# Unused padding tiles in front of the large SBUF tiles of a fused attention and two-MLP kernel

## The chip, the cores and the metric

The kernel runs on one NeuronCore of a Trainium2 chip as one launch. The metric is the device time of that launch in microseconds (us). TensorE (PE in the profile) multiplies, and its weight loads are listed apart as PEld; VectorE (DVE), ScalarE (ACT) and GpSimd (POOL) work on the elements, and SyncE (SP) issues the DMAs. SBUF is the on-chip memory from which the engines read, PSUM the one into which TensorE writes.

## The reference

```python
# 2 batches x 12 heads x 448 tokens x 64, causal
scores = scale * q @ k.T;  scores = where(mask, -1e9, scores)
attn = softmax(scores);    x = attn @ v          # -> x: 896 tokens x 768
h = x @ w_in                                     # 768 x 2048
x = (h * sigmoid(h)) @ w_out                     # 2048 x 768
h = x @ w_in2                                    # 768 x 1024
s = h * softmax(h)                               # over the 1024 features
x = layernorm(s) * g_ln @ w_out2                 # 1024 x 768 -> output 896 x 768
```

All inputs and outputs are float32.

## The kernel before

After the attention come four products, called GEMM1 to GEMM4 here. Each float32 operand is split into a high part and a low part in the type float32r, both four bytes long, and each block product is three matmuls: high by high, and the two mixed ones. A matmul holds one operand in the array as weights (128 rows by 128 columns, the second argument of `nc.tensor.matmul` in this kernel) and streams the other one, the moving operand, past it (128 rows by 256 to 512 columns, the third argument). A weight load of its own (LDWEIGHTS) goes with every matmul, and the profile shows it beside the matmul before it.

- GEMM1 (L295 to L305) has the split weights `wh`, `wl` of `w_in` as array weights, and the attention's result `xh`, `xl` as moving operand, 448 columns for each of the two batches: 16 x 6 x 2 blocks, 576 matmuls. The first 36 of them are issued between pieces of the last heads of the attention (`g1drain`).
- GEMM2 (L479 to L484) has the same ring of weight tiles, and the gated values as moving operand: `gh0`, `gl0` for batch 0 and `gh1`, `gl1` for batch 1, again 448 columns. Its loop takes three blocks (nine matmuls) of batch 0 and then the same three of batch 1; the last four chunks (36 matmuls for each batch) stand apart: first all of batch 0, then all of batch 1. 288 matmuls for each batch.
- GEMM3 (L588 to L597) turns it round: the activations `yh`, `yl` are the array weights, and the whole split matrix `w3h`, `w3l` in SBUF is moving, 512 columns. Seven token tiles of 36 matmuls, 252 in all. Behind each tile, the softmax and layer norm of it run on DVE and ACT.
- GEMM4 (L641 to L652) has transposed activations `lh`, `ll` as array weights and `w4h`, `w4l` as moving operand: 288 matmuls of 384 columns, and in the last token tile 24 of 512 and 24 of 256 columns. The transposes (L630) of a later token tile stand between.

Instructions stand on each engine in the order in which the program is written (`manual_schedule`). The stream of weights is converted and split by ACT, DVE and POOL into a ring of four pairs of tiles ahead of TensorE (`feed_to`, `conv_a`, `conv_b`, `split_w`).

Tile pools lay their tiles one behind the other in each partition of SBUF. Strides and block offsets of all four products are multiples of 256 bytes (448 columns are 1792 bytes, 128 columns 512 bytes, 384 columns 1536 bytes, 768 columns 3072 bytes), so the start of an operand modulo 256 is the same for every block of a product. These are the starts that the built program has:

| product | moving, start mod 256 | weights, start mod 256 | weights minus moving, mod 256 |
|---|---|---|---|
| GEMM1 | `xh`, `xl` 160 | `wh`, `wl` 160 | 0 |
| GEMM2, batch 0 | `gh0`, `gl0` 224 | `wh`, `wl` 160 | 192 |
| GEMM2, batch 1 | `gh1`, `gl1` 160 | `wh`, `wl` 160 | 0 |
| GEMM3 | `w3h`, `w3l` 224 | `yh`, `yl` 160 | 192 |
| transposes of GEMM4 | `ident` 128 | `e` 224 | 96 |
| GEMM4 | `w4h`, `w4l` 160 | `lh`, `ll` 224 | 64 |

The tiles of batch 0 (`gh0`, `gl0`) and `w3h`, `w3l` lie in pools at the right-hand end of SBUF, the others at the left.

Of the kernel before, what the change touches and what calls it, by code (L numbers as in the profile page):

```python
# [8 lines left out]
F32 = mybir.dt.float32  # L9
# [34 lines left out]
def fused(ctx, tc, qT, kT, vv, vt, w1, w2, w3, w4, gl, out):  # L44
# [3 lines left out]
    def pool(name, bufs=1, **kw):  # L48
        return tc.alloc_tile_pool(name=name, bufs=bufs, **kw)

    const = pool("const")
    act = pool("act")
    raw = pool("raw", RAWS)
    xs = pool("xs", XS)
    wring = pool("wring", 4)

    ident = const.tile([128, 128], F32, name="ident")
    xh = act.tile([128, KD, T], F32R, name="xh", tag="ah")
    xl = act.tile([128, KD, T], F32R, name="xl", tag="al")
    g_h, g_l = [None, None], [None, None]  # L60

    with tc.manual_schedule():
# [169 lines left out]
        def split_w(n, c, dst=None, lo_engine=None):  # L232
            x = wx.pop((n, c))
            if dst is None:
                h = wring.tile([128, CH], F32R, name="wh", tag="wh")
                l = wring.tile([128, CH], F32R, name="wl", tag="wl")
                wsp[n, c] = (h, l)
            else:
                h, l = dst
            nc.scalar.activation(h, x, AF.Copy)  # L240
            (lo_engine or nc.gpsimd).tensor_tensor(l, x, h.bitcast(F32), ALU.subtract)  # L241
# [65 lines left out]
        def silu(f, b):  # L307
            ps = gps.pop((f, b))
            sg = sgr.tile([128, S], F32, name="sg", tag="sg")
            nc.scalar.activation(sg, ps[:, :S], AF.Sigmoid)  # L310
            nc.vector.tensor_tensor(sg, ps[:, :S], sg, ALU.mult)
            nc.vector.tensor_copy(g_h[b][:, f], sg)  # L312
            nc.gpsimd.tensor_tensor(g_l[b][:, f], sg, g_h[b][:, f].bitcast(F32), ALU.subtract)  # L313
# [133 lines left out]
        silu(0, 0)  # L447
        silu(1, 0)
        g1p = pool("g1")
        g_h[1] = g1p.tile([128, KF, S], F32R, name="gh1", tag="gh")  # L450
        g_l[1] = g1p.tile([128, KF, S], F32R, name="gl1", tag="gl")
        psd = pool("psd", 2, space=PS)
# [33 lines left out]
        def evict2(ps, d, b):  # L486
            sl = slice(b * S, b * S + S)
            nc.scalar.activation(yh[:, d, sl], ps[:, :S], AF.Copy)
            nc.vector.tensor_tensor(yl[:, d, sl], ps[:, :S], yh[:, d, sl].bitcast(F32), ALU.subtract)
# [3 lines left out]
        def block2(m, b):  # L493
            d, f = divmod(m, KF)
            if f == 0 and b == 0:
                if d < KD - 1:
                    yps[d, 0], yps[d, 1] = pair()
                else:
                    for z in range(B):
                        yps[d, z] = gm.tile([128, 512], F32, name="ps", tag="gm")  # L500
            mm2(yps[d, b], d, f, b)
            return d if f == KF - 1 else None
# [24 lines left out]
        w3p = pool("w3", side="right")  # L527
        w3h = w3p.tile([128, KD * DF2], F32R, name="w3h", tag="h")
        w3l = w3p.tile([128, KD * DF2], F32R, name="w3l", tag="l")
        for m in range(N3):  # L530
            if m == 10:
                for a in tail:
                    block2(a, 1)
                evict2(yps[KD - 1, 1], KD - 1, 1)
            sl = slice(CH * m, CH * m + CH)
            split_w(3, m, (w3h[:, sl], w3l[:, sl]), nc.vector if m % 3 else nc.gpsimd)
# [2 lines left out]
        wring.release()  # L539

        w4p = pool("w4")
        w4h = w4p.tile([128, KF2, DM], F32R, name="w4h", tag="h")
        w4l = w4p.tile([128, KF2, DM], F32R, name="w4l", tag="l")
        dp = pool("dp", 2)

        gain = dp.tile([128, KF2], F32, name="gain", tag="gain", bufs=1)
        nc.sync.dma_start(gain, gl)
# [136 lines left out]
        w4p.release()  # L684
        w3p.release()
        gm.release()
        xs.release()
        raw.release()
        act.release()
# [38 lines left out]
```

## Time and profile before

| | |
|---|---|
| time, median of 3 runs | 449.2 us (448.37 to 449.21) |
| the profiled execution, its own time | 449.83 us |
| its span, first to last instruction | 448.1 us |
| TensorE busy | 440.0 us, 98% |
| VectorE busy | 320.9 us, 72% |
| granted TensorE clock, mean | 0.999 of 2.4 GHz |

The profile is of one execution. Matmuls overlap in the records: a matmul of 448 columns is drawn some 0.37 us long, but the next one starts after some 0.2 us. What a matmul costs is therefore the distance from its start to the start of the next one; it is called its pitch below. The views give starts to 0.01 us, so a pitch is taken over runs of many matmuls.

### The profile page before, as it was taken

Reading aid. Unit: us, or ns where it says so; the run is one execution under the profiler, and the core shown is the slowest. Engines: PE = TensorE matmul, PEld = TensorE weight load, DVE = VectorE, ACT = ScalarE, POOL = GpSimd, SP = SyncE. Lnnn points to the kernel's source line nnn. Section 1 sums busy time; section 2 is a strip of 40 time slices with the busy share of each in tenths; the row PEclk is TensorE's granted clock in tenths of the full one; section 3 lists DMA queues with packets and bytes.
Section 4 is the critical chain, followed back from the end, with each engine's and each line's share of the span. In section 5 each row is a group of like instructions: output and inputs, shape, how many; then the busy total and the mean of one; then the engine's idle time right before and its main releaser. Section 6 shows DMA issues by size and latency. Waiting matters only on the chain.

```text
span 448.1 us, 6969 instructions
## 1 busy us (share of the span) xinstructions
PE 440.0 (98%) x2379; PEld 383.6 (86%) x2379; DVE 320.9 (72%) x705; ACT 223.6 (50%) x519; POOL 168.3 (38%) x197
## 2 busy tenths in 40 slices
PE   8899999999999999999999999999999999999997
PEld 5676767689999999999999999999888888999996
DVE  4988987679999888887785969756878787511110
ACT  4999898354353434344344344433647765712121
POOL 3756664147776656564422424332500000000000
PEclk9999999999999999999999999999999999999999
DMA  5777310205243333333745647464023210010101
GB/s 163 208 244 216 90 37 37 72 27 157 100 140 106 108 95 117 108 106 90 243 126 176 184 149 236 151 198 119 23 71 105 83 60 1 33 39 35 55 35 54
DMA packets 26387, 49.22 MB, mean 110 GB/s; under 512 B 6128, under 2 KB 13936, under 8 KB 26352
## 3 DMA queue, kind: packets, MB, share of 16 engines
q1 hardware_dynamic: 26352, 48.77, 35.2%
q8 instruction: 19, 0.31, 0.3%
q14 instruction: 16, 0.13, 0.1%
HBM read 46.01 MB, written 2.75 MB: 109 GB/s over the span
## 4 chain that ended last, share of the span: by engine, by line
PE 91%; ACT 4%; DVE 4%; issue 0%; DVEq 0%; ACTq 0%
PE h L304 8%; PE h L305 8%; PE h L303 8%; PE h L483 7%; PE h L482 7%; PE h L484 7%; PE ps L650 4%; PE ps L652 4%; PE ps L651 4%; PE h L595 4%; PE h L597 4%; PE h L596 4%; PE pv L186 4%; PE tr L158 3%; ACT e L135 3%; PE sa L118 2%
## 5 line engine op out<-in xcount | busy, mean ns | idle before, releaser
L241 POOL TENSOR_TENSOR wl<-wx,wh 128x384 fp32r<-128x384 f32 x64 | 75.4, 1178 | 102.1 <-ACT wh L240 101.0
L240 ACT ACTIVATE wh<-wx 128x384 fp32r<-128x384 f32 x64 | 33.4, 522 | 77.5 <-PE h L304 37.7
L209 ACT ACTIVATE wr<-wr 128x384 f32<-128x384 f32 x96 | 52.5, 553 | 30.4 <-DMA wr<-w_in 30.4
L220 DVE SCALAR_TENSOR_TENSOR wx<-wr,wx 128x384 uint32<-128x384 uint32 x96 | 65.6, 684 | 0.0
L303 PE MATMUL h<-xh,wh 128*128 128x448 f32 x174 | 64.0, 368 | 0.0
L304 PE MATMUL h<-xl,wh 128*128 128x448 f32 x174 | 64.0, 368 | 0.0
L305 PE MATMUL h<-xh,wl 128*128 128x448 f32 x174 | 64.0, 368 | 0.0
L230 DVE TENSOR_SCALAR wr<-wr 128x384 uint32<-128x384 uint32 x96 | 59.9, 624 | 2.8 <-DMA wr<-w_in 2.7
L214 DVE SCALAR_TENSOR_TENSOR wx<-wr 128x384 uint32<-128x384 uint32 x96 | 59.1, 615 | 1.3 <-POOL gl L313 1.3
L483 PE MATMUL h<-gl,wh 128*128 128x448 f32 x160 | 58.5, 366 | 0.0
L482 PE MATMUL h<-gh,wh 128*128 128x448 f32 x160 | 58.5, 365 | 0.0
L484 PE MATMUL h<-gh,wl 128*128 128x448 f32 x160 | 58.2, 364 | 0.0
L313 POOL TENSOR_TENSOR gl<-sg,gh 128x448 fp32r<-128x448 f32 x32 | 41.2, 1288 | 21.2 <-DVE gh L312 11.3
L135 ACT ACTIVATE e<-e,st 128x384 f32<-128x384 f32 (+3 forms) x84 | 43.6, 523 | 8.3 <-DVE st L129 8.3
L145 POOL TENSOR_TENSOR e<-e,st 128x384 f32<-128x384 f32 (+3 forms) x63 | 37.5, 631 | 26.9 <-PE tr L158 16.6
L650 PE MATMUL ps<-w4h,lh 128*128 128x384 f32 (+2 forms) x112 | 38.3, 342 | 0.0
L651 PE MATMUL ps<-w4l,lh 128*128 128x384 f32 (+2 forms) x112 | 37.8, 338 | 0.0
L652 PE MATMUL ps<-w4h,ll 128*128 128x384 f32 (+2 forms) x112 | 37.8, 337 | 0.0
L639 DVE TENSOR_TENSOR ll<-tp,lh 128x512 fp32r<-128x512 f32 x14 | 9.0, 686 | 38.0 <-ACT lh L638 38.0
L304 PEld LDWEIGHTS h<-xl,wh 128*128 128x128 f32 x174 | 32.7, 188 | 3.4
L303 PEld LDWEIGHTS h<-xh,wh 128*128 128x128 f32 x174 | 32.7, 188 | 3.3
L305 PEld LDWEIGHTS h<-xh,wl 128*128 128x128 f32 x174 | 32.7, 188 | 3.2
(100 smaller groups left out, 845.0 us busy)
## 6 DMA issues: line engine op xcount, KB each, us to landing
wr<-w_in SPq DMA_DIRECT2D x96, 384.0 KB, 3.5
k<-kT_in SPq DMA_DIRECT2D x12, 224.0 KB, 2.8
q<-qT_in SPq DMA_DIRECT2D x12, 192.0 KB, 3.0
v<-vv_in SPq DMA_DIRECT2D x12, 192.0 KB, 2.9
out<-o SPq DMA_DIRECT2D x12, 192.0 KB, 1.9
qt<-qT_in SPq DMA_DIRECT2D x24, 16.0 KB, 2.5
v<-vt_in SPq DMA_DIRECT2D x12, 32.0 KB, 2.5
out<-o SPq DMA_DIRECT2D x1, 256.0 KB, 2.0
```

Of the source, the lines that this page charges most:

```text
L135: nc.scalar.activation(ep(p, u), ep(p, u), AF.Exp, bias=st[p][:, 0, n:n + 1], scale=-1.0, accum_out=st[p][:, 1, n:n + 1])
L214: nc.vector.scalar_tensor_tensor(x.bitcast(U32), r[:, :, 1], 0x80000000, r[:, :, 0], ALU.bitwise_and, ALU.bitwise_or)
L220: nc.vector.scalar_tensor_tensor(xu, r[:, :, 1], 3, xu, ALU.logical_shift_left, ALU.bitwise_or)
L230: nc.vector.tensor_scalar(low, low, 29, None, ALU.logical_shift_right)
L241: (lo_engine or nc.gpsimd).tensor_tensor(l, x, h.bitcast(F32), ALU.subtract)
L303: nc.tensor.matmul(ps[:, :S], wh, rh, start=k == 0, stop=False)
L304: nc.tensor.matmul(ps[:, :S], wh, rl, start=False, stop=False)
L305: nc.tensor.matmul(ps[:, :S], wl, rh, start=False, stop=k == KD - 1)
L482: nc.tensor.matmul(ps[:, :S], wh, rh, start=f == 0, stop=False)
L483: nc.tensor.matmul(ps[:, :S], wh, rl, start=False, stop=False)
L484: nc.tensor.matmul(ps[:, :S], wl, rh, start=False, stop=f == KF - 1)
L650: nc.tensor.matmul(ps[:, :w], lh[:, k], w4h[:, k, ns], start=k == 0, stop=False)
```

## The change

A helper `pad` allocates a tile that nothing writes or reads, so that the tiles behind it in the pool start later. No instruction, no wait and no order on any engine differs between the two programs; only addresses do. A pool `gap` is added so that the tiles behind `xh`, `xl` keep their starts modulo 256 (the raw and converted weights, `wr` and `wx`, move by 64 bytes).

```diff
--- before.py
+++ after.py
@@ -52,9 +52,16 @@
     act = pool("act")
     raw = pool("raw", RAWS)
     xs = pool("xs", XS)
+    gap = pool("gap")
     wring = pool("wring", 4)
 
     ident = const.tile([128, 128], F32, name="ident")
+
+    def pad(where, count):
+        where.tile([128, count // 4], F32, name="pad", tag="pad", bufs=1)
+
+    pad(act, 64)
+    pad(gap, 192)
     xh = act.tile([128, KD, T], F32R, name="xh", tag="ah")
     xl = act.tile([128, KD, T], F32R, name="xl", tag="al")
     g_h, g_l = [None, None], [None, None]
@@ -447,6 +454,7 @@
         silu(0, 0)
         silu(1, 0)
         g1p = pool("g1")
+        pad(g1p, 64)
         g_h[1] = g1p.tile([128, KF, S], F32R, name="gh1", tag="gh")
         g_l[1] = g1p.tile([128, KF, S], F32R, name="gl1", tag="gl")
         psd = pool("psd", 2, space=PS)
@@ -527,6 +535,7 @@
         w3p = pool("w3", side="right")
         w3h = w3p.tile([128, KD * DF2], F32R, name="w3h", tag="h")
         w3l = w3p.tile([128, KD * DF2], F32R, name="w3l", tag="l")
+        pad(w3p, 192)
         for m in range(N3):
             if m == 10:
                 for a in tail:
@@ -539,9 +548,11 @@
         wring.release()
 
         w4p = pool("w4")
+        pad(w4p, 96)
         w4h = w4p.tile([128, KF2, DM], F32R, name="w4h", tag="h")
         w4l = w4p.tile([128, KF2, DM], F32R, name="w4l", tag="l")
         dp = pool("dp", 2)
+        pad(dp, 192)
 
         gain = dp.tile([128, KF2], F32, name="gain", tag="gain", bufs=1)
         nc.sync.dma_start(gain, gl)
@@ -684,6 +695,7 @@
         w4p.release()
         w3p.release()
         gm.release()
+        gap.release()
         xs.release()
         raw.release()
         act.release()
```

The built program's starts with it:

| product | moving, start mod 256 | weights, start mod 256 | distance before | distance now |
|---|---|---|---|---|
| GEMM1 | 224 | 160 | 0 | 192 |
| GEMM2, batch 0 | 224 | 160 | 192 | 192 |
| GEMM2, batch 1 | 224 | 160 | 0 | 192 |
| GEMM3 | 32 | 224 | 192 | 192 |
| transposes of GEMM4 | 128 | 0 | 96 | 128 |
| GEMM4 | 0 | 0 | 64 | 0 |

The tiles of the attention itself keep their distances.

## Rows read from the trace of the kernel before

**Rows 1.** The page: busy time; the chain that ended last; groups (busy, mean ns | idle).
```profile
PE 440.0 (98%) x2379; PEld 383.6 (86%) x2379; DVE 320.9 (72%) x705; ACT 223.6 (50%) x519; POOL 168.3 (38%) x197
...
PE 91%; ACT 4%; DVE 4%; issue 0%; DVEq 0%; ACTq 0%
...
L303 PE MATMUL h<-xh,wh 128*128 128x448 f32 x174 | 64.0, 368 | 0.0
...
L482 PE MATMUL h<-gh,wh 128*128 128x448 f32 x160 | 58.5, 365 | 0.0
```

**Rows 2.** Busy time by stretch: GEMM1's start and middle, GEMM2, GEMM3, GEMM4.
```profile
core 0: us, PE busy (x) PEld busy (x) DVE busy (x) ACT busy (x) POOL busy (x), PEclk, DMA share, GB/s
...
94.00:114.00 20.00, 20.00 (x98) 18.17 (x97) 19.75 (x30) 8.55 (x18) 14.67 (x12) 1.00 0.39 119
130.00:190.00 60.00, 60.00 (x292) 54.51 (x291) 52.80 (x83) 24.25 (x50) 38.12 (x33) 1.00 0.36 111
205.00:315.00 110.00, 110.00 (x543) 101.57 (x542) 82.75 (x153) 45.34 (x90) 37.59 (x32) 1.00 0.56 171
321.00:380.00 59.00, 59.00 (x260) 48.09 (x260) 45.78 (x101) 36.56 (x63) 5.11 (x7) 1.00 0.19 61
381.00:445.00 64.00, 63.87 (x379) 62.38 (x377) 11.49 (x21) 18.52 (x34) 0.93 (x2) 1.00 0.12 42
```

**Rows 3.** Timeline of PE in GEMM1: start us, us, instruction; nine matmuls apart.
```profile
149.97 0.37 PE L303 MATMUL h<-xh,wh 128*128 128x448 f32 x1
...
151.83 0.37 PE L303 MATMUL h<-xh,wh 128*128 128x448 f32 x1
```

**Rows 4.** Timeline of PE in GEMM2's loop: where the batch changes.
```profile
249.63 0.37 PE L482 MATMUL h<-gh,wh 128*128 128x448 f32 x1
...
251.49 0.36 PE L482 MATMUL h<-gh,wh 128*128 128x448 f32 x1
...
253.29 0.37 PE L482 MATMUL h<-gh,wh 128*128 128x448 f32 x1
```

**Rows 5.** Timeline of PE in GEMM2's last four chunks: batch 0, batch 1, GEMM3's first.
```profile
306.39 0.36 PE L482 MATMUL ps<-gh,wh 128*128 128x448 f32 x1
...
313.59 0.37 PE L482 MATMUL ps<-gh,wh 128*128 128x448 f32 x1
...
321.03 0.39 PE L595 MATMUL h<-w3h,yh 128*128 128x512 f32 x1
```

**Rows 6.** Timeline of PE in the attention's last pieces: GEMM1's second nine, to a transpose.
```profile
83.08 0.36 PE L303 MATMUL ps<-xh,wh 128*128 128x448 f32 x1
...
84.90 0.27 PE L158 MATMUL tr<-ident,e 128*128 128x128 f32 x1
```

**Rows 7.** Timeline of PE in GEMM3: begin of tiles 2, 3, 4, 6; last tile's second matmul.
```profile
329.28 0.39 PE L595 MATMUL h<-w3h,yh 128*128 128x512 f32 x1
...
337.53 0.40 PE L595 MATMUL h<-w3h,yh 128*128 128x512 f32 x1
...
345.93 0.40 PE L595 MATMUL h<-w3h,yh 128*128 128x512 f32 x1
...
362.73 0.40 PE L595 MATMUL h<-w3h,yh 128*128 128x512 f32 x1
...
371.12 1.04 PE L630 MATMUL tp<-ident,e 128*128 128x128 f32 x8
...
372.23 0.40 PE L596 MATMUL h<-w3l,yh 128*128 128x512 f32 x1
...
380.26 0.27 PE L630 MATMUL tp<-ident,e 128*128 128x128 f32 x1
```

**Rows 8.** Timeline of PE in GEMM4: nine apart at 384, 512 and 256 columns.
```profile
385.90 0.34 PE L650 MATMUL ps<-w4h,lh 128*128 128x384 f32 x1
...
387.49 0.34 PE L650 MATMUL ps<-w4h,lh 128*128 128x384 f32 x1
...
436.38 0.39 PE L650 MATMUL ps<-w4h,lh 128*128 128x512 f32 x1
...
438.48 0.39 PE L650 MATMUL ps<-w4h,lh 128*128 128x512 f32 x1
...
443.01 0.28 PE L650 MATMUL ps<-w4h,lh 128*128 128x256 f32 x1
...
444.03 0.28 PE L650 MATMUL ps<-w4h,lh 128*128 128x256 f32 x1
```

**Rows 9.** Timeline of POOL and PE where GEMM1's third output block (f = 2) begins.
```profile
97.11 1.14 POOL L241 TENSOR_TENSOR wl<-wx,wh 128x384 fp32r<-128x384 f32 x1
...
100.16 0.37 PE L305 MATMUL h<-xh,wl 128*128 128x448 f32 x1
```

## The prediction

> **What bounds the kernel now.** I read the page first, for the bound: TensorE is busy 440.0 of 448.1 us, and the chain that ended last runs through PE for 91% of the span; the other engines hold it only inside the attention [rows 1]. So from GEMM1 on, time can only go or come by what a matmul costs on TensorE. A busy share doesn't say that, since a matmul's record overlaps the next one's. The second view, busy time by stretch, says it by counts: in GEMM1's middle, 60 us touch 292 matmuls (the first two began earlier), so about one in 207 ns; GEMM2 fits 543 into 110 us, about one in 203 ns, although its matmuls have the same 448 columns [rows 2]. The granted clock is 1.00 in all these stretches, the level of 2.4 GHz, so no clock explains the difference.
>
> The third view, the timeline of PE alone, shows where it comes from. In GEMM1 nine matmuls take 1.86 us: a pitch of 206.7 ns [rows 3]. In GEMM2's loop the nine of batch 1 take 1.86 us too, and the nine of batch 0 behind them 1.80 us: 200.0 ns [rows 4]. It is the same line with the same ring of weights, the same shape, and the page has no idle time before such a line [rows 1]; what differs is the tile that is streamed. The last four chunks repeat it in long runs: 36 matmuls of batch 0 take 7.20 us (200.0 ns), the 36 of batch 1 behind them 7.44 us (206.7 ns) [rows 5]. The table of starts puts a number on the tiles: batch 0 begins 64 bytes off the weights modulo 256 (distance 192), batch 1 and all of GEMM1 at the same residue (distance 0). The program before thus holds a trial of the change in itself.
>
> **The change part by part.** Nothing is added to any engine, no wait is new, nothing is moved past anything. Only starts change, so each product is priced by matmuls times difference in pitch.
>
> GEMM1 goes from distance 0 to 192, with exactly the residues of GEMM2's batch 0 (224 moving, 160 weights). Of its 576 matmuls 540 run back to back and set the end; 540 x 6.7 ns = 3.6 us less. The 36 at the start lie between pieces of the attention. There the pitch at distance 0 is irregular and lower, 1.82 us for nine or 202.2 ns [rows 6], so they would give between 36 x 2.2 and 36 x 6.7 ns, 0.1 to 0.2 us, and less where the attention's chain waits for other engines; I take 0.
>
> GEMM2's batch 1 goes from 0 to 192: 288 x 6.7 ns = 1.9 us less. Batch 0 stays as it is.
>
> Can the weights follow? The tightest place is early in GEMM1: from 94 to 114 us DVE, which converts them, is busy 19.75 of 20 us [rows 2]. The split that feeds the third output block ends at 98.25 us, and TensorE first reads it at 100.16 us: 1.9 us to spare [rows 9]. Until there TensorE has issued the first two blocks of both batches, 72 matmuls, worth at most 72 x 6.7 = 0.5 us, so the cover holds with 1.4 us left. In GEMM1's middle DVE is busy 52.80 of 60 us, in GEMM2 82.75 of 110 [rows 2]: room for a TensorE that is 3% faster. If the cover fails from 94 to 130 us, the gain of that stretch is lost, 36 us / 206.7 ns = 174 matmuls, 1.2 us. That end lies inside the range.
>
> GEMM3 keeps its distance of 192, though both starts change. It has two pitches in itself: its 36 matmuls take 8.25 us in tiles one and two, 8.40 and 8.39 us in tiles three and six (four and five are like them), and in the last tile 35 take 8.03 us: 229.2, 233.3 and 229.4 ns [rows 5, 7]. No address differs modulo 256 between these tiles, so the pitch also depends on how the stream came into step. Taken as it is: 0. All tiles at the low pitch would give 144 x 4.1 ns = 0.6 us, all at the high one would cost 108 x 4.1 ns = 0.4 us.
>
> GEMM4 goes from 64 to 0, a distance that the trace shows only at 448 columns. At 64 the pitch is 176.7 ns for 384 columns (1.59 us for nine), 233.3 for 512 and 113.3 for 256 [rows 8]. Half way between 384 and 512, 448 columns would take 205.0 ns at distance 64, against 206.7 at distance 0 [rows 3]; by that the change costs 1.7 ns x 336 = 0.6 us. From the other side: the 256-column matmuls run at 113.3 / 256 = 0.443 ns a column, and 384 columns at that rate take 170.0 ns, 6.7 less, so 288 x 6.7 = 1.9 us to win if distance 0 lets them. Both rows lie equally far (one differs in distance, the other in width), so I take the middle, 0.7 us less. As far ends I keep the whole difference that distance made in GEMM2, either way: 336 x 6.7 = 2.3 us. The 56 transposes in front go from 96 to 128; at 6.7 ns each that is 0.4 us either way, and I take 0.
>
> A rule of the Trainium skill speaks against all of it. "TensorE: Matmul & The Clock Gate", in "Step-by-step: what each phase is for", says that TensorE reads streamed operand and weights through two independent ports, and that loading the next weights doesn't take read bandwidth from the running matmul. By it the sum would be 0, and the same page, in "Wait — 56ns, not 53.3ns?", gives a pitch of columns over 2.4 GHz plus some 2.5 ns; my estimate from that is 189 ns for 448 columns. The trace agrees with neither: 200.0 and 206.7 ns stand side by side [rows 4].
>
> The sum: 3.6 + 1.9 + 0.7 = 6.2 us less. The profiled execution took 449.83 us, 1.7 of it around its span of 448.1; it would take 443.6. It lies 0.6 us above the median of the three runs, 449.2, so for a median the forecast is 443.0 us.
>
> **The rivals.**
>
> First, GEMM1 falls out of step. GEMM3's third tile shows that a stream at distance 192 can change to a higher pitch and stay there, here over four tiles [rows 7], which in GEMM1 would mean 206.7 ns as before. Against it: the longest run at 192 with 448 columns, 36 matmuls, holds 200.0 ns without a break, and every group of nine begins with it at once [rows 4, 5]. Left are GEMM2's 1.9 and GEMM4's 0.7 us: 446.6.
>
> Second, the distance isn't the cause. `gh0` and `gl0` lie at the right-hand end of SBUF, `gh1`, `gl1`, `xh` and `xl` at the left, so the trial in the trace also compares places. Then padding does nothing: 449.2. Against it speaks that `w3h`, `w3l` lie on the right as well and show both pitches [rows 7]. This is also where the rule of the skill leads.
>
> Third, slower: the high pitch is the state into which any unbroken stream settles, and GEMM2's batch 0 is low only because a stream at another distance ends every nine matmuls before it. With one distance for both batches nothing breaks the stream any more, and from the first tens of matmuls GEMM2's batch 0 takes 206.7 ns: 288 x 6.7 = 1.9 us more. The rest of GEMM3 settles too (0.4), and GEMM4 pays its 0.6: 2.9 us in all, 452.1. For it speaks that GEMM1 is irregular and lower at its start [rows 6] and steady at 206.7 later; against it, the unbroken 36 [rows 5]. It decides if a stream needs more than 36 matmuls to settle.
>
> Fourth, GEMM4 gains more than the bound, because distance 0 suits 384 columns better than 192 suits 448: each further nanosecond there is 0.3 us, and the time falls below 440.
>
> **How the numbers follow.** Forecast with its bounds, 78%; fourth rival, 4%; first, 7%; second, 6%; third, 5%. The low end of the range: 3.6 + 1.9 + 0.2 (the first 36) + 2.3 (GEMM4) + 0.6 (GEMM3) + 0.4 (transposes) = 9.0 us less, 440.2, and 440.0 with half of the spread of the runs, 0.4 us. The high end: GEMM1 and GEMM2 as counted (5.5), GEMM4 2.3 and GEMM3 0.4 worse: 2.8 us less, 446.4. The 18% outside are the second and third rival, the fourth, and most of the first. A measurement of this kernel can tell about 0.2% (0.9 us) from no change. Forecast, first and fourth rival lie beyond that: faster 89%; within it the second, 6%; slower the third, 5%.
>
> **What the profile after would show.** Nine matmuls of GEMM1 in 1.80 us instead of 1.86, at any place from 95 us on; no difference between GEMM2's batches; GEMM2 beginning 3.6 us earlier than now, GEMM3 5.5. In GEMM4 nine matmuls of 384 columns between 1.53 and 1.61 us, with 1.59 meaning that distances 0 and 64 are alike. The count of instructions and the waits of PE in GEMM1 and GEMM2 (none now) stay. The forecast is wrong if GEMM1 still takes 1.86 us for nine (first or second rival, which GEMM2's batch 1 tells apart), if batch 0 rises to 1.86 (third), or if idle time appears in front of PE in GEMM1, which would mean that the split weights come late.

## The result and the profile after

The changed kernel takes 442.5 us (median of four runs, 442.3 to 443.0), the one before 449.0 us beside it: a ratio of 0.986, 95% interval 0.9842 to 0.9877. The forecast was 443.0 us. The profiled execution went from 449.83 to 442.50 us, its span from 448.1 to 440.7.

Timeline of PE in the changed kernel, which answers to [rows 3, 5] (L310 is the former L303, L490 the former L482, L606 the former L595): first two rows 45 matmuls apart in GEMM1, then the last four chunks of GEMM2.

```profile
144.76 0.36 PE L310 MATMUL h<-xh,wh 128*128 128x448 f32 x1
...
153.76 0.36 PE L310 MATMUL h<-xh,wh 128*128 128x448 f32 x1
...
300.76 0.36 PE L490 MATMUL ps<-gh,wh 128*128 128x448 f32 x1
...
307.96 0.36 PE L490 MATMUL ps<-gh,wh 128*128 128x448 f32 x1
...
315.16 0.39 PE L606 MATMUL h<-w3h,yh 128*128 128x512 f32 x1
```

9.00 us for 45 is 200.0 ns, where GEMM1 had 206.7; both batches take 7.20 us for 36, where batch 1 had 7.44. The same view at the borders of the stages, in the kernel before and then in the changed one (first matmul of GEMM1 and of GEMM2; first of GEMM4 and the last of all; GEMM3's first is in the fence above and in [rows 5]):

```profile
74.14 0.47 PE L303 MATMUL ps<-xh,wh 128*128 128x448 f32 x1
...
203.91 0.36 PE L482 MATMUL h<-gh,wh 128*128 128x448 f32 x1
...
381.05 0.42 PE L650 MATMUL ps<-w4h,lh 128*128 128x384 f32 x1
...
444.60 0.28 PE L652 MATMUL ps<-w4h,ll 128*128 128x256 f32 x1
```

```profile
73.88 0.47 PE L310 MATMUL ps<-xh,wh 128*128 128x448 f32 x1
...
199.96 0.36 PE L490 MATMUL h<-gh,wh 128*128 128x448 f32 x1
...
374.55 0.42 PE L661 MATMUL ps<-w4h,lh 128*128 128x384 f32 x1
...
437.28 0.28 PE L663 MATMUL ps<-w4h,ll 128*128 128x256 f32 x1
```

| stretch | before, us | after, us | gain | forecast |
|---|---|---|---|---|
| attention, to GEMM1's first | 74.14 | 73.88 | 0.3 | 0 |
| GEMM1 | 129.77 | 126.08 | 3.7 | 3.6 |
| GEMM2 | 117.12 | 115.20 | 1.9 | 1.9 |
| GEMM3 and its transposes | 60.02 | 59.39 | 0.6 | 0 |
| GEMM4 to its last matmul | 63.55 | 62.73 | 0.8 | 0.7 |

The 0.3 us of the attention can't be told from its spread: in the fourteen traces of this case GEMM1's first matmul starts between 73.2 and 74.9 us.

Busy time by stretch, early GEMM1, its middle, and GEMM2, against [rows 2]: 302 matmuls stand in GEMM1's 60 us instead of 292, and DVE's share there rose from 52.80 to 56.55 us, since the same conversions now have less time.

```profile
94.00:114.00 20.00, 20.00 (x102) 18.75 (x101) 19.75 (x30) 8.30 (x18) 14.93 (x12) 1.00 0.40 119
130.00:190.00 60.00, 60.00 (x302) 56.24 (x301) 56.55 (x88) 25.68 (x54) 41.96 (x35) 1.00 0.40 119
205.00:310.00 105.00, 105.00 (x527) 98.42 (x526) 80.25 (x150) 42.78 (x87) 35.93 (x29) 1.00 0.58 173
```

The tightest feed, against [rows 9]: the split now ends at 97.95 us (96.81 + 1.14) and is first read at 99.56: 1.6 us to spare instead of 1.9.

```profile
96.81 1.14 POOL L248 TENSOR_TENSOR wl<-wx,wh 128x384 fp32r<-128x384 f32 x1
...
99.56 0.36 PE L312 MATMUL h<-xh,wl 128*128 128x448 f32 x1
```

### The profile page after: what moved, and what is told of

Read it like the earlier page. It is cut to its first block, busy times and chain, and to the rows that moved or that the text cites. A ratio compares the mean times of both kernels' runs of the same rounds, so it can differ in the third digit from the quotient of the medians.

```text
span 440.7 us, 6969 instructions
## 1 busy us (share of the span) xinstructions
PE 432.4 (98%) x2379; PEld 382.2 (87%) x2379; DVE 321.9 (73%) x705; ACT 223.5 (51%) x519; POOL 170.3 (39%) x197
## 4 chain that ended last, share of the span: by engine, by line
PE 91%; ACT 4%; DVE 4%; issue 0%; DVEq 0%; ACTq 0%
PE h L312 8%; PE h L311 8%; PE h L310 8%; PE h L492 7%; PE h L491 7%; PE h L490 7%; PE ps L663 4%; PE ps L661 4%; PE ps L662 4%; PE h L608 4%; PE h L607 4%; PE h L606 4%; PE pv L193 4%; PE tr L165 3%; ACT e L142 3%; PE sa L125 2%
## 5 line engine op out<-in xcount | busy, mean ns | idle before, releaser
L248 POOL TENSOR_TENSOR wl<-wx,wh 128x384 fp32r<-128x384 f32 x64 | 77.6, 1212 | 95.4 <-ACT wh L247 91.8
L227 DVE SCALAR_TENSOR_TENSOR wx<-wr,wx 128x384 uint32<-128x384 uint32 x96 | 66.6, 694 | 0.0
L311 PE MATMUL h<-xl,wh 128*128 128x448 f32 x174 | 63.1, 362 | 0.0
L310 PE MATMUL h<-xh,wh 128*128 128x448 f32 x174 | 62.6, 360 | 0.0
L490 PE MATMUL h<-gh,wh 128*128 128x448 f32 x160 | 57.6, 360 | 0.0
L310 PEld LDWEIGHTS h<-xh,wh 128*128 128x128 f32 x174 | 32.5, 187 | 2.3
```

Source lines behind the costliest of these rows:

```text
L227: nc.vector.scalar_tensor_tensor(xu, r[:, :, 1], 3, xu, ALU.logical_shift_left, ALU.bitwise_or)
L310: nc.tensor.matmul(ps[:, :S], wh, rh, start=k == 0, stop=False)
L311: nc.tensor.matmul(ps[:, :S], wh, rl, start=False, stop=False)
L490: nc.tensor.matmul(ps[:, :S], wh, rh, start=f == 0, stop=False)
```

## The experiments

All but the two timed ones are single profiled runs, read by their pitches: the mean time from a matmul's start to the next one's, over a product or a batch in the trace, steps from one batch to the other taken in. The longer steps where a tile of GEMM3 or GEMM4 begins are left out. GEMM1's means take in its irregular first 36 matmuls: 206.5 ns there is 206.7 from 110 to 190 us. The granted clock is 0.999 or 1.000 of 2.4 GHz in every trace. The edits of the sizes are to the changed kernel; "224/160" below means a stream that starts at 224 and weights at 160, modulo 256.

**Shift both.** `gap` and the padding of `g1p` go, `xh` stays moved (not shown in the cut: GEMM4's paddings become 32 and 128).

```diff
     pad(act, 64)
-    pad(gap, 192)
...
-        pad(g1p, 64)
```

> The padding in front of xh stays, but the weights ring and gh1 move by the same 64 bytes: GEMM1 and both batches of GEMM2 stream from residue 224, as in the changed kernel, at distance 0. Theory (the distance decides): 206.7 ns in GEMM1 and in both batches, so batch 0, the one that was low before the change, rises from 200.0 too; GEMM2 is 1.9 us longer than before, the whole kernel 1 to 2 us slower than before less what GEMM3 and GEMM4 give. Rival (the residue 224 of the streamed tile decides): 200.0 in all three. Rival (the place of gh0 decides): batch 0 at 200.0, the others at 206.7. GEMM3 keeps its residues of the changed kernel (32 and 224, distance 192): if its low pitch belongs to them, all seven tiles take 229 ns; if chance brings it in step, some tiles may take 233. GEMM4 stands at 192: if 192 is the best distance whatever the width, its 384 columns take less than 173.5 ns; if the best distance hangs on the width, more.

Batch 0 rose, so neither its place nor the residue of the stream made its 200 ns. But the pitch is 202.6 ns, not 206.7, in all three; 445.2 us. The rows are the tail of GEMM2: 7.29 and 7.30 us for 36.

```profile
303.10 0.36 PE L488 MATMUL ps<-gh,wh 128*128 128x448 f32 x1
...
310.39 0.36 PE L488 MATMUL ps<-gh,wh 128*128 128x448 f32 x1
...
317.69 0.40 PE L604 MATMUL h<-w3h,yh 128*128 128x512 f32 x1
```

GEMM3 ran at 229.0 ns in all seven tiles, apart from two steps of 0.32 and 0.34 us where the third begins, GEMM4 at 173.2 for 384 columns.

**Two sweeps of distances.** Sizes of the paddings in bytes, not program lines, in the order act, gap, g0 (a new padding behind `gl0`), g1, w3, w4, dp.

```diff
-64, 192,   0,  64, 192, 96, 192   # changed kernel
+64,  64, 224, 128,   0, 96,  64   # first sweep
+64, 128,  96,  96,  64, 96, 224   # second sweep
```

> Distances that no run has shown: GEMM1 at 64, GEMM2 batch 0 at 32, batch 1 at 128, GEMM3 at 0, GEMM4 at 128. Theory A (only a near-equal start clashes): GEMM1 and batch 1 at 200 ns or less, batch 0 between 200 and 206.7, GEMM3 at 233 or more, GEMM4 at 173 or less. Theory B (the pattern repeats every 128 bytes, so that 128 is like 0 and 64 like 192): GEMM1 200, batch 1 206.7, GEMM4 at 128 like at 0, 173.5. If neither holds, each distance has a pitch of its own and 256 is the period.

> The rest of the sweep: GEMM1 at 128, GEMM2 batch 0 at 224, batch 1 at 160, GEMM3 at 64, GEMM4 at 32. The distance theory wants GEMM1 here to have the pitch that batch 1 has at 128 in the run before it (within 0.3 ns), although other tiles are streamed. Theory A: all three at or below 203 ns. Theory B: GEMM1 206.7, batch 0 like a distance of 96. GEMM4 at 32 lies between 173.5 (at 0) and 176.7 (at 64) if the pitch changes smoothly.

| distance | 448 columns, ns (stream/weights) | 512 columns, GEMM3 | 384, GEMM4 | 256, GEMM4 |
|---|---|---|---|---|
| 0 | 206.7 (160/160), 202.6 (224/224) | 227.1 | 173.7 | 119.7 |
| 32 | 203.3 (0/32) | | 173.8 | 118.0 |
| 64 | 202.2 (224/32) | 233.3 | 176.7 | 113.8 |
| 128 | 204.0 (224/96), 203.4 (160/32; 204.0 in the unbroken 36) | | 176.0 | 118.4 |
| 160 | 205.7 (192/96) | | | |
| 192 | 200.0 (224/160) | 229.0 | 173.2 | 117.8 |
| 224 | 206.1 (128/96) | | | |

Neither theory A nor B holds: there is no single clash point, 128 isn't like 0, and the order differs by width (0 is the best of the three at 512 columns and, from 160/160, the worst of all at 448; 64 is the best at 256 columns only). At 384 columns 0, 32 and 192 are not to be ranked: behind the first six or so steps of a tile all three run at 173.3 ns. GEMM1 alone, streaming from 224, had 202.2, 204.0, 200.0 and 202.6 ns with weights at 32, 96, 160 and 224: with the stream's start kept, the start of the weights moves its pitch.

Over the whole of batch 1 the distance theory misses its test at 128 (203.4 ns against GEMM1's 204.0, with 0.3 allowed). But that is a broken stream: batch 0, at another distance, stands between every nine of its matmuls. In its unbroken 36 batch 1 settles on 204.0, GEMM1's pitch, from other starts, and so at 128 the theory stands. Thirty matmuls take 6.12 us in both, batch 1 (first sweep) first, then GEMM1 (second):

```profile
311.68 0.37 PE L491 MATMUL ps<-gh,wh 128*128 128x448 f32 x1
...
317.80 0.37 PE L491 MATMUL ps<-gh,wh 128*128 128x448 f32 x1
```

```profile
146.14 0.36 PE L310 MATMUL h<-xh,wh 128*128 128x448 f32 x1
...
152.26 0.36 PE L310 MATMUL h<-xh,wh 128*128 128x448 f32 x1
```

**192 elsewhere.** The same distance from other starts, 160/96 in GEMM1 and GEMM2.

```diff
-    pad(act, 64)
...
+        pad(g0p, 64)
...
-        pad(w3p, 192)
...
-        pad(w4p, 96)
+        pad(w4p, 160)
```

> Distance 192 everywhere in GEMM1 and GEMM2, but from other starts: 160 streamed and 96 for the weights, where all 200.0 ns so far came from 224 and 160. Theory (the distance decides): 200.0 ns in GEMM1 and in both batches. Rival (the pair of starts decides, as distance 0 at 160 and 160 with 206.6 and at 224 and 224 with 202.6 suggests): another pitch, 202 to 207.

200.0 ns in GEMM1 and in both batches; 441.8 us. At 192 the distance did decide, for both pairs of starts tried.

```profile
144.11 0.36 PE L309 MATMUL h<-xh,wh 128*128 128x448 f32 x1
...
153.11 0.36 PE L309 MATMUL h<-xh,wh 128*128 128x448 f32 x1
```

**GEMM1 undone**, four timed runs.

```diff
-    pad(act, 64)
-    pad(gap, 192)
...
-        pad(w3p, 192)
```

> GEMM1's part of the change undone (distance 0, both starts at 160 as before), the rest kept, and GEMM3 at the starts of before (224 and 160). If the starts decide: GEMM1 at 206.6 ns again, both batches of GEMM2 at 200.0, 3.6 us more than the changed kernel, 446.1 us. If GEMM1's 206.7 before was a state that it fell into by chance: 202.6 ns as at 224 and 224, 443.9 us. GEMM3: if its high pitch before was bound to its starts, tiles three to six take 8.40 us again; if it came from how the stream came into step, it may take 8.25 in all.

446.5 us, ratio to before 0.9949 (0.9929 to 0.9969): GEMM1 was back at 206.5 ns, both batches stayed at 200.0. Its median lies 4.0 us above the changed kernel's, for the 3.6 us at which GEMM1 was priced; the spread of its four runs is 1.3. All five traces with GEMM1 at 160/160 have this pitch, and all four at distance 192 have 200.0, so it isn't a state that one execution fell into. Here 45 matmuls take 9.30 us:

```profile
146.81 0.37 PE L308 MATMUL h<-xh,wh 128*128 128x448 f32 x1
...
156.11 0.37 PE L308 MATMUL h<-xh,wh 128*128 128x448 f32 x1
```

GEMM3, at its starts of before, settled on 229.0 ns in every tile: its high pitch of [rows 7] is no property of its starts. The third tile still took 8.35 us, by a step of 0.34 us at its begin, but the next two 8.24 each and not 8.40.

```profile
335.59 0.50 PE L603 MATMUL h<-w3h,yh 128*128 128x512 f32 x1
335.93 0.39 PE L604 MATMUL h<-w3l,yh 128*128 128x512 f32 x1
```

**Distance 0 at two more starts.** All of GEMM1 to GEMM3 at 192/192 and at 96/96.

```diff
-64, 192,   0, 64, 192,  96, 192   # changed kernel
+32,   0,  32,  0,  32,  64, 192   # 192/192
+192,  0, 128,  0, 128, 160, 192   # 96/96
```

> Distance 0 in GEMM1, GEMM2 and GEMM3 with all starts at 192. So far distance 0 had 206.5 ns with starts at 160 (three kernels) and 202.6 with starts at 224 (one). If the starts modulo 64 matter (160 and 224 are both 32 past a multiple, 192 is one), a third pitch is possible; if distance 0 simply has two states, one of the two is seen, 202.6 or 206.5. GEMM3 at distance 0: 227 ns as in the two runs with starts at 224, if the distance decides.

> Distance 0 with all starts at 96, which is 32 past a multiple of 64 like 160 and 224. If the pair of starts modulo 128 decided, 96 would be like 224 and take 202.6 ns; if distance 0 has two states, 202.6 or 206.5, and the stages of one run need not agree. GEMM3 at 227 ns if the distance decides.

At 192/192 GEMM1 had 206.5 ns and both batches 206.7 (450.0 us), at 96/96 all three 202.7 (444.9 us); GEMM3 227.2 and 227.0. With 160 and 224 that fits a rule by starts modulo 128 (96 there: 202.6; 32 and 64: 206.7), on four starts and no more. The tails, first 192/192, then 96/96:

```profile
308.09 0.37 PE L489 MATMUL ps<-gh,wh 128*128 128x448 f32 x1
...
315.53 0.37 PE L489 MATMUL ps<-gh,wh 128*128 128x448 f32 x1
```

```profile
303.20 0.37 PE L489 MATMUL ps<-gh,wh 128*128 128x448 f32 x1
...
310.50 0.36 PE L489 MATMUL ps<-gh,wh 128*128 128x448 f32 x1
```

**Standing reads**, on the kernel before: the weights alone, the stream alone, both (the cut shows both lines; each of the first two runs has one of them).

```diff
             wh, wl = wblock(2, d * KF + f)
+            wh, wl = (a[:, :1].to_broadcast([128, 128]) for a in (wh, wl))
             rh, rl = g_h[b][:, f], g_l[b][:, f]
+            rh, rl = (a[:, :1].to_broadcast([128, S]) for a in (rh, rl))
```

> The kernel before, but GEMM2's weight loads read the first of the 128 columns 128 times over (step 0), so that they stay at one address; starts are those of before. It computes other values from GEMM2 on. Theory (the weight read, walking through SBUF, meets the walking stream): the pitches of the batches, 200.0 and 206.7, both change, and come to within 1 ns of each other if the walk alone makes the clash. Rival (what counts is when a load starts, not what it reads): 200.0 and 206.7 as before.

> The kernel before, but in GEMM2 the stream reads its first column 448 times over (step 0) while the weight loads walk as before; other values from GEMM2 on. If the clash needs two walking reads or a walking stream, both batches lose their excess over 186.7 ns (448 columns at 2.4 GHz), to 190 or less. If the stream's own start address decides alone, 200.0 and 206.7 stay. If a walking weight load meets a standing stream now and then, something between, and the same in both batches.

> Both reads of GEMM2 stand still: stream and weight load each read one column over and over, in batch 0 at starts 192 apart modulo 256, in batch 1 at the same start modulo 256; other values from GEMM2 on. Theory (the memory is divided by address modulo 256, and two reads of one part at once cost time): batch 1 pays most, above 206.7 ns, batch 0 nothing, below 192. Rival (no such division; the excess is a cost of stepping into the stream): both batches alike.

Weights standing: 203.6 ns in batch 0, 206.0 in batch 1; both changed, but the excess stayed and the batches came no closer than 2.4 ns. Stream standing: 189.2 ns in batch 0 and 189.1 in batch 1, and the same again with both standing. So it is the walking stream that loses time. That two standing reads at the same start lose nothing was against the theory of a divided memory as I put it; it doesn't refute one, if a stream that stays on one column needn't read the memory anew for each, which no run here tells. Stream standing, the two tails (6.81 us for 36 each):

```profile
299.26 0.35 PE L483 MATMUL ps<-gh,wh 128*128 128x448 f32 x1
...
306.07 0.35 PE L483 MATMUL ps<-gh,wh 128*128 128x448 f32 x1
...
312.88 0.40 PE L596 MATMUL h<-w3h,yh 128*128 128x512 f32 x1
```

These three kernels leave GEMM4 as it was, and show a second pitch there at unchanged starts (160/224, distance 64): in each, the first of the six tiles of 384 columns settles on 173.3 ns, the other five on 176.7, where the kernel before had 176.7 in all six. Eighteen matmuls with the stream standing in GEMM2, in the first tile and then in the second:

```profile
376.52 0.34 PE L651 MATMUL ps<-w4h,lh 128*128 128x384 f32 x1
...
379.64 0.34 PE L651 MATMUL ps<-w4h,lh 128*128 128x384 f32 x1
...
385.80 0.34 PE L651 MATMUL ps<-w4h,lh 128*128 128x384 f32 x1
...
388.98 0.34 PE L651 MATMUL ps<-w4h,lh 128*128 128x384 f32 x1
```

**Half the weights** in GEMM4 (one of its three matmul lines shown; the other two, the copy and the store are cut to 64 in the same way).

```diff
-                    nc.tensor.matmul(ps[:, :w], lh[:, k], w4h[:, k, ns], start=k == 0, stop=False)
+                    nc.tensor.matmul(ps[:64, :w], lh[:, k, :64], w4h[:, k, ns], start=k == 0, stop=False)
...
```

> GEMM4 loads 64 of the 128 weight columns for each matmul and so computes and writes the first 64 of every 128 tokens alone; all else as in the changed kernel. At 2.4 GHz 384 columns are 160.0 ns, so its 173.5 ns hold 13.5 ns of excess. Theory (the excess comes from reads of the next weights that meet the stream): half the weights, half the excess, 165 to 168 ns. Rival (the excess is a cost of every matmul, or of the stream alone): 173.5 as before. The Trainium skill's TensorE: Matmul & The Clock Gate (Step-by-step: what each phase is for) stands on the rival's side.

175.0 ns on average at 384 columns, settled at 173.3 in three tiles and at 176.7 in the three between them: not less. At 256 columns 113.7 against 119.7. The excess is not in proportion to the weights that a load reads.

**Two distances tuned further**, four timed runs.

```diff
-        pad(w3p, 192)
...
-        pad(dp, 192)
+        pad(dp, 128)
```

> The changed kernel with two distances moved to what the sweep showed lowest: GEMM3 at 0 (227.1 ns in the sweep against 229.0) and GEMM4 at 192 (173.2 ns at 384 columns against 173.7). If a pitch belongs to its starts: 252 x 1.9 + 288 x 0.5 = 0.6 us less than the changed kernel, 441.9 us. If GEMM3 falls into its high pitch: 1 us more.

442.25 us (441.96 to 442.69), ratio to before 0.9856 (0.984 to 0.9871). GEMM3 had 226.9 ns and GEMM4 173.2, as the sweep said; GEMM3 with its transposes fell by 0.3 us to 59.05, where 252 x 2.1 ns = 0.5 was due, and GEMM4 by 0.1. Some 0.2 us were lost again at the third tile's start, where PE's timeline shows steps of 0.30 and 0.34 us instead of 0.23:

```profile
331.78 0.39 PE L607 MATMUL h<-w3h,yl 128*128 128x512 f32 x1
332.08 0.50 PE L605 MATMUL h<-w3h,yh 128*128 128x512 f32 x1
332.42 0.39 PE L606 MATMUL h<-w3l,yh 128*128 128x512 f32 x1
```

Its total can't be told from that of the changed kernel (442.5 us).

## Why the prediction was right

- GEMM1 and GEMM2: the trial that the trace held was the right one. The step "540 x 6.7 ns" gave 3.6 us, measured 3.7; "288 x 6.7 ns" 1.9, measured 1.9. Batch 0 kept 7.20 us, so its low pitch wasn't a product of breaks (third rival), and left-hand tiles took 200.0 ns (second). GEMM1's 540 stayed in step (first).
- The cover: the weights' feed had 1.6 us left where 1.4 were forecast, and PE has no wait there. That GEMM2 began 3.95 us and GEMM3 5.87 us earlier, and not 3.6 and 5.5, is the attention's 0.3 us above all.
- GEMM4: the forecast of 0.7 us came near the measured 0.8, but it was the middle of two bounds, neither of which came, so that it lay so near is luck. The upper one (0.6 us of loss, from GEMM1's 206.7) leaned on a wrong step: that distance 0 costs at 384 columns what it costs at 448. The lower one (1.9 us to win) took 384 columns down to 170.0 ns, the rate per column of 256; no run has them settle below 173.3. Distance 0 gave 173.7 ns for 176.7 at 384 columns (288 x 3.0 = 0.9), 228.5 for 233.3 at 512 (0.1) and cost at 256 (119.7 for 113.8, 0.1).
- GEMM3: priced at 0, measured 0.6 less, the low end of its bound (144 x 4.1 ns). The runs give no ground to credit it to the change: at the starts of before, five kernels of the experiments ran GEMM3 at 228.9 to 229.1 ns. The two profiled executions differ by 7.3 us and the medians by 6.5; this 0.6 us would be most of the reason if the other executions of the kernel before had the low pitch, which isn't shown, since no trace shows them.
- Named too simply: "distance" was taken as the cause. It did decide at 192 and at 128 (two pairs of starts each), but at 0 the starts themselves move the pitch by 4 ns. Nor do starts settle it alone at every width: at unchanged starts GEMM3 had 229.2 and 233.3 ns, and GEMM4's 384 columns 173.3 and 176.7. At 448 columns, where 5.5 of the forecast 6.2 us lay, no pair of starts settled on two pitches in these traces. That GEMM1 and batch 1 began at 160, where 0 is costly, made the change worth its full price; from 224/224 to 192 the same step would have been 2.6 ns a matmul.
- The rule of two independent ports in the Trainium skill ("TensorE: Matmul & The Clock Gate", "Step-by-step: what each phase is for"): where the stream stood still, the estimate of 189 ns from that page ("Wait — 56ns, not 53.3ns?") was met at 189.2, with walking weight loads beside it. For a walking stream no pair of starts came below 200.0, and moving the weights alone shifted the pitch, for which that rule leaves no room.

Open: what in the memory or in TensorE's sequence of loads makes a walking stream pay, why the order of distances differs by width, and what picks one of two pitches at unchanged starts (each change between them falls at the start of a tile). Standing weights and half weights changed the pitch without removing the excess, so a plain count of meetings with the weight read isn't shown.

## What to carry to other kernels

Where TensorE runs without idle time, read the pitch, start to start, and compare products of one shape over stretches that nothing breaks: a difference with no wait in it can lie in the starts of the operands, and a padding that costs nothing can take it away. Price it by width and by pair of starts from the trace of the kernel at hand, not by a rule of distance, and take the best pair that two or three profiled runs show.

## What was unexpected in the hardware

The pitch settles into patterns that repeat every three or five matmuls (at 224/160: 197, 202, 201 ns; at 224/224: 203, 202, 203, 199, 207). GEMM3 at one pair of starts showed two of them in one execution, 229.2 and 233.3 ns [rows 7], with no start changed modulo 256 between; GEMM4 did the same at 384 columns. The whole excess of a 448-column matmul over a standing stream, 206.7 less 189.2, is 17.5 ns, and the change recovers 6.7 of it.
